# Experts on pairs of 256 slots with seven half-size products in a gated recurrence and mixture-of-experts kernel

## The chip, the cores and the metric

The kernel runs on one core of a Trainium2 chip. A core has a matrix engine (TensorE, PE in the profile), a vector engine (VectorE, DVE), a scalar engine (ScalarE, ACT), GpSimd (POOL) and a queue engine for transfers (SyncE, SP). They run side by side and wait for each other by semaphores. Matmul results go to PSUM, which has eight banks of 512 f32 columns on 128 partitions; everything else on the chip lies in SBUF. The metric is the device time of one execution in microseconds. All arithmetic is f32.

## The reference, cut to what matters

A gated linear recurrence over 768 steps makes 3072 rows of 384 features. A router picks two of eight experts for each row; each expert is a two-layer network, and its result is weighted and added.

```python
f = 1.0 / (1.0 + np.exp(-f_logit))                     # B, H, S, D = 4, 8, 768, 48
for t in range(S):
    state = f[:, :, t, :, None] * state + np.einsum('bhd,bhe->bhde', k[:, :, t], v[:, :, t])
    y[:, :, t] = np.einsum('bhd,bhde->bhe', q[:, :, t], state)
x = y.transpose(0, 2, 1, 3).reshape(B * S, H * D)       # 3072 x 384

noisy_logits = x @ w_gate + np.log1p(np.exp(x @ w_noise)) * noise
top2 = np.argpartition(-noisy_logits, 2, axis=1)[:, :2] # top2_w: softmax over the two
for e in range(E):                                      # E = 8, w1[e] 384 x 1024, w2[e] 1024 x 384
    for k in range(2):
        mask = top2[:, k] == e
        h = np.maximum(x[mask] @ w1[e], 0.0)
        out[mask] += top2_w[mask, k, None] * (h @ w2[e])
```

So there are 6144 slots (a row and one of its experts), and in the expert part almost all the arithmetic lies: 24 + 24 weight tiles of 128 x 128 per expert. On the given inputs the experts get 766, 738, 811, 777, 800, 755, 719 and 778 slots.

## The kernel before

The attention works through 24 steps (six chunks of 128 time steps for each of four batch rows). In every step VectorE, ScalarE and TensorE take turns; the loads of f, q, k and v go into rings of padded tiles:

```python
RING = {"f": 5, "q": 4, "k": 4, "v": 6}
pads = {n: [ld.tile([C, H, DP], F32, tag=f"{n}{i}", name=f"{n}{i}") for i in range(RING[n])] for n in "fqkv"}
```

The router of each chunk ranks the slots and writes each expert's list of slots to memory. After half of the chunks a first plan (`NA` = 17 blocks) and after all of them a second plan say which expert and which 128 slots each of the 48 blocks takes; four half blocks of 64 slots take what is left of a list. The first blocks begin while the attention's last steps still run. A block is this:

```python
def turned(t):
    xp = one_bank(f"xgp{t}")
    for i in range(KO):                                   # KO = 3
        nc.tensor.transpose(xp[:, i * 128:(i + 1) * 128], xg[t][:, i * 128:(i + 1) * 128], ident)
    xt[t] = ffn.tile([128, KO, 128], F32, tag="xt", name=f"xt{t}")
    nc.vector.tensor_copy(xt[t], xp[:, 0:DM].rearrange("d (k t) -> d k t", k=KO))

def block_of(t, end=NB - NT):
    ahead("fetch", min(t + 5, end))                       # slot lists of later blocks
    ahead("gather", min(t + 4, end))                      # their rows, by an indirect DMA
    hs = ffn.tile([128, FO, 128], F32, tag="hs", name=f"hs{t}")
    for half in range(2):
        hp = one_bank(f"hp{t}_{half}").rearrange("f (o t) -> f o t", t=128)
        for o in range(FO // 2):                          # FO = 8
            fo = half * (FO // 2) + o
            for i in range(KO):
                nc.tensor.matmul(hp[:, o, :], lhsT=w1[t % NR][:, i, fo * 128:(fo + 1) * 128],
                                 rhs=xt[t][:, i, :], start=(i == 0), stop=(i == KO - 1))
        nc.scalar.activation(hs[:, half * (FO // 2):(half + 1) * (FO // 2), :], hp, AF.Relu)
        # ... (the pieces take turns with other work: yield)
    ahead(1, min(t + NR + 1, end))                        # w1 of block t + 2, if its expert is another
    if t + 1 < end:
        turned(t + 1)
    yield
    yp = one_bank(f"yp{t}")
    for fo in range(FO):
        nc.tensor.matmul(yp[:, 0:DM], lhsT=hs[:, fo, :], rhs=w2[t % NR][:, fo, :],
                         start=(fo == 0), stop=(fo == FO - 1))
        # ...
    ahead(2, min(t + NR + 1, end))                        # w2 of block t + 2
    ys = ffn.tile([128, DM], F32, tag="ys", name=f"ys{t}")
    nc.vector.tensor_scalar(ys, yp[:, 0:DM], slots[t][:, 1:2].bitcast(F32), None, ALU.mult)
    nc.gpsimd.indirect_dma_start(out=out, out_offset=bass.IndirectOffsetOnAxis(ap=slots[t][:, 2:3], axis=0),
                                 in_=ys, in_offset=None, bounds_check=N - 1, oob_is_err=False, compute_op=ALU.add)
    yield
```

The last transfer scatters the block's weighted rows into `out` and adds them there. The half block does the same with 64 slots, on both column halves of TensorE, and ends in two scatters. A branch behind the main part takes what the plan could not place; on these inputs it isn't taken.

Of the kernel before, what the change touches and what calls it, by code (L numbers as in the profile page):

```python
# [331 lines left out]
def kernel(  # L332
# [37 lines left out]
    nc = tc.nc  # L370
# [10 lines left out]
    NB = max((2 * N - 65 * n) // 128 + n for n in range(E + 1))  # L381
    NH = 4
    HALF = NCH // 2
    NT = 3
    NA = -(-(2 * HALF * B * C - E * 127) // 128)
# [12 lines left out]
    ps2 = ctx.enter_context(tc.tile_pool(name="ps2", bufs=1, space=PSUM))  # L398
    ps1 = ctx.enter_context(tc.tile_pool(name="ps1", bufs=6, space=PSUM))
    wk = ctx.enter_context(tc.tile_pool(name="wk", bufs=2))  # L400
    ffn = ctx.enter_context(tc.tile_pool(name="ffn", bufs=3))
    loads = ExitStack()
    ld = loads.enter_context(tc.tile_pool(name="ld", bufs=1))

    def one_bank(name):
        return ps1.tile([128, 512], F32, tag="one", name=name)
# [10 lines left out]
    pads = {n: [ld.tile([C, H, DP], F32, tag=f"{n}{i}", name=f"{n}{i}") for i in range(RING[n])] for n in "fqkv"}  # L417
# [16 lines left out]
    end_of = counting("end_of", [[128, N // 128]], base=128)  # L434
    block = counting("block", [[1, NB]])

# [10 lines left out]
    LR = E * N + 128  # L447
# [42 lines left out]
    xw, puts = [], []  # L490
# [123 lines left out]
    def route(c):  # L614
# [63 lines left out]
        def put(b, r):  # L678
            into = nc.gpsimd.indirect_dma_start(  # L679
# [15 lines left out]
    steer, steer_h = {}, {}  # L695

    def plan(name, n, groups, count):


        def t(shape, tag, dtype=F32):  # L700
            return rt.tile([128] + shape, dtype, tag=tag, name=f"{tag}_{name}", bufs=1)

        total = one_bank(f"total_{name}")[:, 0:E]
        nc.tensor.matmul(total, lhsT=ones, rhs=upto[groups - 1][:, :, B], start=True, stop=True)
        full = t([E, N // 128], "full")
        nc.vector.tensor_tensor(full, total.unsqueeze(2).broadcast_to((128, E, N // 128)),
                                (end_of if count == ALU.is_ge else over_of).unsqueeze(1).broadcast_to((128, E, N // 128)), count)
        yield
        nblk, ends, step = t([E], "nblk"), t([E], "ends"), t([E], "step")
        nc.vector.tensor_reduce(nblk, full, axis=AX.X, op=ALU.add)  # L710
        if count == ALU.is_gt:
            half, first, ends_h = t([E], "half"), t([E], "first"), t([E], "ends_h")
# [30 lines left out]
        yield  # L743
        nc.vector.memset(new[:, 0:NR], 1.0)
        nc.vector.tensor_tensor(new[:, NR:], ex[:, NR:], ex[:, 0:n - NR], ALU.not_equal)
        nc.vector.tensor_copy(to[:, :, 2], new)
        yield
        if count == ALU.is_ge:

# [375 lines left out]
```

## Time and profile before

| what | value |
|---|---|
| time, median of three runs | 725.64 us (725.5 to 729.05) |
| span of the profiled execution | 730.0 us, mean TensorE clock 0.984 |
| first-layer matmuls (line 838), x2304 | 267.7 us |
| second-layer matmuls (line 849), x768 | 257.3 us |
| turning of gathered rows (line 816), x144 | 24.0 us |
| scatters into `out` (line 856), x48 | 76.0 us on GpSimd |
| weights, inputs and outputs through the hardware queue | 135.91 MB |

In the profile's lines a name such as L838 is a line of the kernel. A line of the slices gives for each fortieth of the span the busy share of an engine in tenths. A row of the timeline has the start, the duration, the engine, the line, the operation with its output and inputs, and how many instructions were merged; in brackets stands how long the engine had been idle and who ended that. A row by stretch of time gives the stretch, its length, the busy time of PE, of the weight loads, of DVE, ACT and POOL, then the clock, the share of the DMA engines that was busy, and GB/s. A row of waits gives who waited for whom, the sum in us, how many times, and the longest.

### The profile page before, as it was taken

How to read it: one execution, taken by the hardware profiler on the slowest of the kernel's cores; microseconds unless marked ns; L12 is line 12 of the kernel's file. 1: busy time of each engine (PE TensorE's matmuls, PEld its weight loads, DVE VectorE, ACT ScalarE, POOL GpSimd, SP SyncE). 2: the span in 40 equal slices, each digit the busy share in tenths (PEclk: the TensorE clock that was granted, in tenths of full speed). 3: DMA queues.
4: the chain of work that ended last, by engine and by line, in shares of the span. 5: the costliest groups of instructions: out<-in, count | busy, mean ns of one | idle time of the engine just before them, and what ended most of it. 6: DMA issues, size and time to landing. Idle time of an engine off the chain costs nothing.

```text
span 730.0 us, 13666 instructions
## 1 busy us (share of the span) xinstructions
PE 699.4 (96%) x5354; PEld 563.0 (77%) x5354; DVE 200.2 (27%) x503; ACT 163.7 (22%) x365; POOL 232.8 (32%) x267
## 2 busy tenths in 40 slices
PE   6999989969999999999999999999999999999992
PEld 5889978858788787787788768876787678767881
DVE  7878887822232250010110110010011001101000
ACT  5766655621111010110010011001110101010100
POOL 5223674421174562122132123312322232312210
PEclk9999999989999999999999999999999999999997
DMA  8889888889997988899839649974997189563211
GB/s 173 151 199 216 166 164 182 165 279 368 373 260 194 251 189 264 282 301 331 276 57 381 195 113 292 351 250 118 302 348 233 26 267 333 161 210 74 34 23 15
DMA packets 179866, 156.41 MB, mean 214 GB/s; under 512 B 116978, under 2 KB 164240, under 8 KB 179792
## 3 DMA queue, kind: packets, MB, share of 16 engines
q1 hardware_dynamic: 167440, 135.91, 62.7%
q0 software_dynamic: 12352, 19.52, 13.2%
q8 instruction: 45, 0.74, 0.4%
q14 instruction: 29, 0.24, 0.1%
HBM read 192.51 MB, written 20.15 MB: 291 GB/s over the span
## 4 chain that ended last, share of the span: by engine, by line
PE 87%; DMA 5%; DVE 3%; ACT 1%; SPq 1%; issue 1%; POOL 0%; POOLq 0%; DVEq 0%; ACTq 0%
PE hp L838 36%; PE yp L849 34%; PE sc L554 3%; PE xgp L816 2%; PE xp L605 2%; PE y L572 2%; PE yp_h L910 1%; PE hp_h L896 1%; DMA k<-in_k_dram 1%; DMA w<-in_moe_w_dram 1%; DMA x_rows<-xs 1%; PE y L583 1%; DVE L L528 1%; PE kp L514 1%; PE kp L548 1%
## 5 line engine op out<-in xcount | busy, mean ns | idle before, releaser
L838 PEld LDWEIGHTS hp<-xt,w 128*128 128x128 f32 x2304 | 264.9, 192 | 15.3 <-issue 3.4
L838 PE MATMUL hp<-xt,w 128*128 128x128 f32 x2304 | 267.7, 276 | 0.4 <-DMA w<-in_moe_w_dram 0.4
L849 PE MATMUL yp<-w,hs 128*128 128x384 f32 x768 | 257.3, 487 | 0.0
L849 PEld LDWEIGHTS yp<-w,hs 128*128 128x128 f32 x768 | 141.7, 190 | 90.0 <-issue 2.6
L856 POOL DMA_INDIRECT out_dram<-ys,slots x48 | 76.0, 1583 | 308.8 <-DVE ys L855 171.4
L840 ACT ACTIVATE hs<-hp 128x512 f32<-128x512 f32 x96 | 57.3, 597 | 455.1 <-PE hp L838 455.1
L818 DVE COPY xt<-xgp 128x384 f32<-128x384 f32 x48 | 26.8, 558 | 236.8 <-PE xgp L816 236.8
L855 DVE TENSOR_SCALAR ys<-yp,slots 128x384 f32<-128x384 f32 x48 | 29.6, 617 | 204.0 <-PE yp L849 199.4
L799 POOL DMA_INDIRECT xg<-x_rows,slots x48 | 47.9, 999 | 35.4 <-DMA slots<-lists 19.1
L679 POOL DMA_INDIRECT lists<-entry,sloti x48 | 47.6, 992 | 12.9 <-issue 9.1
L508 POOL TENSOR_SCALAR f<-f 128x384 f32<-128x384 f32 x22 | 28.0, 1272 | 30.8 <-DMA f<-in_f_logit_dram 17.4
L557 DVE TENSOR_TENSOR A<-sc,causal 128x1024 f32<-128x1024 f32 x24 | 29.3, 1222 | 16.1 <-PE sc L554 15.9
L554 PE MATMUL sc<-qP,kQ 64*128 64x128 f32 x384 | 30.6, 304 | 0.0
L528 DVE TENSOR_TENSOR_SCAN L<-f,cap 128x512 f32<-128x512 f32 x24 | 29.8, 1243 | 2.2 <-ACT cap L523 2.2
L572 PE MATMUL y<-A,v 128*64 128x128 f32 x384 | 28.1, 290 | 1.7 <-DMA v<-in_v_dram 1.4
L816 PE MATMUL xgp<-ident,xg 128*128 128x128 f32 x144 | 24.0, 276 | 5.5 <-DMA xg<-x_rows,slots 5.5
L915 POOL DMA_INDIRECT out_dram<-ys_h,slots_h x8 | 11.4, 1431 | 55.6 <-DVE ys_h L913 48.0
L554 PEld LDWEIGHTS sc<-qP,kQ 64*128 64x128 f32 x384 | 25.7, 204 | 4.3 <-issue 3.8
L605 PE MATMUL xp<-w_rt,yT 128*128 128x112 f32 x192 | 27.2, 284 | 0.0
L572 PEld LDWEIGHTS y<-A,v 128*64 128x64 f32 x384 | 21.9, 143 | 5.6 <-DVE A L557 1.6
L605 PEld LDWEIGHTS xp<-w_rt,yT 128*128 128x128 f32 x192 | 23.3, 191 | 3.6 <-issue 2.2
L587 ACT COPY yT<-y 128x256 f32<-128x256 f32 x48 | 15.5, 376 | 41.7 <-PE y L583 40.3
(169 smaller groups left out, 439.3 us busy)
## 6 DMA issues: line engine op xcount, KB each, us to landing
w<-in_moe_w_dram SPq DMA_DIRECT2D x96, 1536.0 KB
w_h<-in_moe_w_dram SPq DMA_DIRECT2D x8, 1536.0 KB
f<-in_f_logit_dram SPq DMA_DIRECT2D x24, 192.0 KB
q<-in_q_dram SPq DMA_DIRECT2D x24, 192.0 KB
k<-in_k_dram SPq DMA_DIRECT2D x24, 192.0 KB
v<-in_v_dram SPq DMA_DIRECT2D x24, 192.0 KB
x_rows<-xs SPq DMA_DIRECT2D x24, 192.0 KB
out_dram<-zero SPq DMA_DIRECT2D x24, 192.0 KB
```

Source lines behind the costliest of these rows:

```text
L528: nc.vector.tensor_tensor_scan(L[n], data0=logf[n], data1=cap[n % 2].rearrange("d a t -> d (a t)"), initial=0.0, op0=ALU.add, op1=ALU.min)
L554: nc.tensor.matmul(sc[:, par, cols(hp)], lhsT=kQ[n][rows(par), cols(hp)], rhs=qP[n][rows(par), cols(hp)], start=True, stop=True)
L572: nc.tensor.matmul(at(hp, par), lhsT=vt[:, 2 * hp + par, :], rhs=A[n][:, par, cols(hp)], start=(hp < 2), stop=(c == 0 and hp >= HP - 2))
L605: nc.tensor.matmul(xp[:, hp, :], lhsT=yT[n][:, hp % 2, cols(hp // 2)], rhs=w_rt[:, hp, :], start=True, stop=True)
L679: into = nc.gpsimd.indirect_dma_start(out=lists, out_offset=bass.IndirectOffsetOnAxis(ap=sloti[:, r, b:b + 1], axis=0), in_=entry[:, c, b, ...
L799: nc.gpsimd.indirect_dma_start(out=xg[t], out_offset=None, in_=x_rows[0:HALF * B * C] if t < NA else x_rows, in_offset=bass.IndirectOffset ...
L816: nc.tensor.transpose(xp[:, i * 128:(i + 1) * 128], xg[t][:, i * 128:(i + 1) * 128], ident)
L838: nc.tensor.matmul(hp[:, o, :], lhsT=w1[t % NR][:, i, fo * 128:(fo + 1) * 128], rhs=xt[t][:, i, :], start=(i == 0), stop=(i == KO - 1))
L840: nc.scalar.activation(hs[:, half * (FO // 2):(half + 1) * (FO // 2), :], hp, AF.Relu)
L849: nc.tensor.matmul(yp[:, 0:DM], lhsT=hs[:, fo, :], rhs=w2[t % NR][:, fo, :], start=(fo == 0), stop=(fo == FO - 1))
L855: nc.vector.tensor_scalar(ys, yp[:, 0:DM], slots[t][:, 1:2].bitcast(F32), None, ALU.mult)
L856: nc.gpsimd.indirect_dma_start(out=out, out_offset=bass.IndirectOffsetOnAxis(ap=slots[t][:, 2:3], axis=0), in_=ys, in_offset=None, bounds_ ...
```

## The change

Blocks of 128 slots become pairs of 256. The first layer keeps its 24 matmuls per pair, each with 256 columns, so that each weight tile is loaded into TensorE half as often. The second layer is a product of a 256 x 1024 by a 1024 x 384 matrix. It is cut in halves in each dimension, and the two-by-two product is formed with seven half-size products instead of eight (Winograd's form of Strassen's scheme), four matmuls of 192 columns each, with VectorE making four sums of hidden quarters (`sm`, S1 to S4), four of weight quarters (`u`) and eight sums of the products:

```diff
+        def mix(*which):
+            for m in which:
+                x, y, op = {"u1": (b(0, 1), b(0, 0), ALU.subtract), "u2": (b(1, 1), u[1], ALU.subtract),
+                            "u3": (b(1, 1), b(0, 1), ALU.subtract), "u4": (b(1, 0), u[2], ALU.subtract),
+                            "s1": (a(0, 1), a(1, 1), ALU.add), "s2": (sm[1], a(0, 0), ALU.subtract),
+                            "s3": (a(0, 0), a(0, 1), ALU.subtract), "s4": (a(1, 0), sm[2], ALU.subtract)}[m]
+                nc.vector.tensor_tensor((u if m[0] == "u" else sm)[int(m[1])], x, y, op)
+        when = [["u3"], ["u1"], ["u2", "s3"], ["u4"]] if t else [[], [], [], ["u3", "s3"]]
+        when += [["s1"], ["s2"], ["s4"]] if t else [["u1", "u2"], ["u4", "s1"], ["s2"]]
...
+        hs = ffn.tile([128, FO, 256], F32, tag="hs", name=f"hs{t}", bufs=1)
+        for fo in range(0, FO, 2):
+            hp = one_bank(f"hp{t}_{fo}").rearrange("f (o t) -> f o t", o=2)
+            for o in range(2):
                 for i in range(KO):
...
+                    nc.tensor.matmul(hp[:, o, :], lhsT=w1[t % NR][:, i, (fo + o) * 128:(fo + o + 1) * 128], rhs=xt[t][:, i, :],
+                                     start=(i == 0), stop=(i == KO - 1))
+            nc.scalar.activation(hs[:, fo:fo + 2, :], hp, AF.Relu)
+            mix(*when[fo // 2])
...
+        def product(name, x, y):
+            if len(P) % 2 == 0:
+                bank.append(one_bank(f"y{t}_{len(bank)}"))
+            P[name] = bank[-1][:, (len(P) % 2) * HC:(len(P) % 2 + 1) * HC]          # HC = 192
+            for o in range(FH):                                                     # FH = 4
+                nc.tensor.matmul(P[name], lhsT=x[:, o, :], rhs=y[:, o, :], start=(o == 0), stop=(o == FH - 1))
+        ys = [ffn.tile([128, DM], F32, tag=f"ys{s}", name=f"ys{t}_{s}", bufs=1) for s in range(2)]
...
+        def scatter(s):
+            nc.scalar.mul(ys[s], ys[s], slots[t][:, s, 1:2].bitcast(F32))
+            nc.gpsimd.indirect_dma_start(out=out, out_offset=bass.IndirectOffsetOnAxis(ap=slots[t][:, s, 2:3], axis=0),
+                                         in_=ys[s], in_offset=None, bounds_check=N - 1, oob_is_err=False, compute_op=ALU.add)
+        product(1, a(0, 0), b(0, 0));  mix(*when[4])                                # (lines joined here)
+        product(7, sm[3], u[3])
+        nc.scalar.copy(P17.rearrange("t a w -> t (a w)"), bank[0][:, 0:DM]);  turned(t + 1, 0);  mix(*when[5])
+        product(2, a(1, 0), b(1, 0));  mix(*when[6])
+        product(4, a(1, 1), u[4])
+        nc.vector.tensor_tensor(left[0], P17[:, 0], P[2], ALU.add)
+        nc.vector.tensor_tensor(left[1], P17[:, 1], P[4], ALU.add);  turned(t + 1, 1)
+        product(5, sm[1], u[1])
+        product(6, sm[2], u[2])
+        nc.vector.tensor_tensor(mid, P17[:, 0], P[6], ALU.add)
+        nc.vector.tensor_tensor(right[1], P17[:, 1], P[5], ALU.add)
+        nc.vector.tensor_tensor(left[1], left[1], mid, ALU.add)
+        nc.vector.tensor_tensor(right[1], right[1], mid, ALU.add)
+        scatter(1)
+        nc.vector.tensor_tensor(mid, mid, P[5], ALU.add)
+        product(3, sm[4], b(1, 1))
+        ahead(2, t + NR + 1)
+        nc.vector.tensor_tensor(right[0], mid, P[3], ALU.add)
+        scatter(0)
```

The eight sums are not given room of their own; they lie in the rings that held f, q and k, which are free once the attention's last loads are used:

```diff
+    f_all = ring.tile([C, RING["f"], H, DP], F32, tag="f_all", name="f_all")
+    qk_all = ring.tile([C, RING["q"] + RING["k"], H, DP], F32, tag="qk_all", name="qk_all")
+    sm = {i + 1: f_all[:, i].rearrange("p h d -> p (h d)").rearrange("p (o t) -> p o t", t=128) for i in range(4)}
+    u = {i + 1: qk_all.rearrange("p a h d -> p (a h d)")[:, i * FO // 2 * HC:(i + 1) * FO // 2 * HC].rearrange(
+        "p (o c) -> p o c", c=HC) for i in range(4)}
```

Therefore all but the first three pieces of the first pair wait for the last steps, and the first plan has five pairs (`NA`), the whole 24 (`NP`):

```diff
-            if early and stage not in (summed, decays):
-                next(blocks)
+            for _ in range(2 if i >= NS - 1 else 1):
+                if done[2] >= NR and (n_first < 3 or i >= NS - 2 and stage is not forget):
+                    next(pairs)
+                    n_first += 1
```

After the attention its PSUM pools are closed and one pool of eight banks takes their place (before: six single banks and one double one throughout). The plan makes pairs, single blocks and half blocks; the main part runs pairs and half blocks only, and single blocks would go to the branch behind it.

## The prediction

> **What bounds the kernel now.** I read the page's busy shares and slices first, to find the engine and the stages.
>
> ```profile
> PE 699.4 (96%) x5354; PEld 563.0 (77%) x5354; DVE 200.2 (27%) x503; ACT 163.7 (22%) x365; POOL 232.8 (32%) x267
> PE   6999989969999999999999999999999999999992
> DVE  7878887822232250010110110010011001101000
> PEclk9999999989999999999999999999999999999997
> ```
>
> TensorE (PE) is busy in nearly every slice at full clock. VectorE (DVE) is busy only in the first eight slices, which are the attention; after that it has room. A busy PE is not a PE at its peak, so I asked for TensorE's waits from 147 us on, and for busy times by stretch.
>
> ```profile
> PE xgp L816 <- DMA xg<-x_rows,slots: 5.5, 1, 5.5
> PE hp L838 <- DMA w<-in_moe_w_dram: 0.4, 1, 0.4
> ...
> 147.00:180.00 33.00, 27.09 (x250) 22.18 (x249) 7.34 (x21) 6.20 (x18) 3.94 (x4) 0.90 0.93 321
> ...
> 300.00:420.00 120.00, 120.00 (x743) 96.34 (x743) 13.62 (x24) 13.14 (x22) 29.27 (x23) 1.00 0.81 261
> 420.00:640.00 220.00, 220.00 (x1342) 167.28 (x1342) 23.81 (x43) 25.65 (x43) 60.47 (x47) 1.00 0.76 234
> ```
>
> From 147 us to the last matmul TensorE waits 5.9 us in all (the first two lines), just where the experts begin. So from 153 to 717 us the time is the sum of TensorE's work, and a change is worth what it takes off that sum, plus what it adds in waits. What one block costs is read from the starts in the timeline of two blocks.
>
> ```profile
> 310.45 5.52 PE L838 MATMUL hp<-xt,w 128*128 128x128 f32 x48
> ...
> 315.80 0.49 PE L816 MATMUL xgp<-ident,xg 128*128 128x128 f32 x3
> ...
> 316.13 5.33 PE L849 MATMUL yp<-w,hs 128*128 128x384 f32 x16
> ...
> 321.29 5.52 PE L838 MATMUL hp<-xt,w 128*128 128x128 f32 x48
> ```
>
> Start to start: first layer 315.80 - 310.45 = 5.35 us, turning the next rows 0.33, second layer 321.29 - 316.13 = 5.16; a block is 10.84 us, two are 21.68. One matmul of the program is two instructions here (24 give x48, 8 give x16), so an instruction takes 5.35/48 = 111.5 ns with 128 columns and 5.16/16 = 322.5 ns with 384.
>
> [...] the transposes show (0.33/3 = 110 ns), while the first layer shows 111.5. [...] the trace has 689 ns for the 128x512 product of line 540. [...] Here every scatter into `out` is ordered that way, and the trace shows it between the two scatters of a half block:
>
> ```profile
> 434.91 1.43 POOL L915 DMA_INDIRECT out_dram<-ys_h,slots_h  x1 [12.01 <-DVE ys_h L913]
> 438.41 1.41 POOL L915 DMA_INDIRECT out_dram<-ys_h,slots_h  x1 [2.07 <-DMA out_dram<-ys_h,slots_h]
> ```
>
> **The change part by part.**
>
> *Amount of work.* On these inputs the eight lists hold 766, 738, 811, 777, 800, 755, 719 and 778 slots. Three pairs serve each, the last one where it has over 192 slots to take; 811, 777, 800 and 778 leave 43, 9, 32 and 10, which are half blocks; no expert leaves a single block. So 24 pairs and four half blocks replace 48 blocks and four half blocks, and the slow branch at the end stays untaken.
>
> *First layer.* 24 matmuls a pair, now with 256 columns: 48 instructions x [...] = 10.36 us, against 2 x 5.35 = 10.70. Off: 0.34 us.
>
> *Second layer.* Seven products of four matmuls with 192 columns: 56 instructions x [...] = 9.10 us, against 10.32. Off: 1.22 us, a little less than an eighth[...]. The six transposes stay, 0.66 us.
>
> So a pair is 20.12 us instead of 21.68: 1.56 us less, times 24 = 37.4 us off TensorE. Half blocks and attention keep their matmuls.
>
> *VectorE.* Per pair: four sums of w2 quarters [...], four of hidden quarters [...], eight sums of products [...], two copies of turned rows at the trace's 558 ns (1.12 us). Sum 10.6 us[...], in 20.1: 53%, beside TensorE. On ScalarE four Relu of 597 ns, a copy and two scalings at about 476 ns (128x384, line 610): 3.8 us. GpSimd: two gathers at 999 ns and two scatters at 1583 ns, 5.2 us, as before for two blocks.
>
> *Do the sums come in time?* From the end of the first layer a product is 1.30 us. The Relu and S1 end at about 0.7 + 0.7 = 1.4 us and S1 is first used by the fifth product at 5.9. S2 waits behind the first turned copy (2.9 to 3.5) and ends near 4.2; it is used at 7.2. S4 ends near 4.9 and is used at 8.5. The sums of w2 and S3 go beside the next pair's first layer: 4 x 0.96 + 0.69 = 4.5 us in 10.4. I find no stop in the steady state.
>
> *Weights.* A set is loaded when it differs from that of two pairs ago: 21 times against 30, 3.1 MB each, 28 MB less. Each half of a set (w1, w2) has 20 us or more to land; the first one took 150.97 to 159.87 us.
>
> *The start.* Blocks start at 153 us now, as the attention's last steps run. The first pair comes at nearly the same place, its slot lists a few slots earlier, but it needs two gathers and operand rings that the attention has just left. I put down 2 us more idle time, bubbles of the first pairs included.
>
> *The tail.*
>
> ```profile
> 717.23 0.62 DVE L855 TENSOR_SCALAR ys<-yp,slots 128x384 f32<-128x384 f32 x1 [9.90 <-PE yp L849]
> 718.12 1.56 POOL L856 DMA_INDIRECT out_dram<-ys,slots  x1 [8.96 <-DVE ys L855]
> ```
>
> Now one scatter goes out 0.9 us after the last matmul. After the change two do. The first needs four sums (about 1.3 us) and a scaling (0.5) after the sixth product, with handovers about 2.5 us, and takes at least 4.2 us to land (the fastest landing of line 856). The second may go only then: 6.7 us after the sixth product, or 5.4 after the seventh. The tail grows by 4.5 us.
>
> Sum: 725.6 - 37.4 + 2 + 4.5 = 694.7; I say 695.
>
> **Rivals.** (a) *VectorE sets the pace.* [...] it would be half busy where it was about a tenth busy (13.62 of 120 us). Against it stand the margins of 2 us or more above. One microsecond lost a pair would cost 24: 719, nothing gained worth the name. (b) *The start eats it.* VectorE is still 70 to 80% busy in the attention, and the first pair's eight sums stand in the same queue; the half used rings and banks change hands just there. Ten more microseconds idle would give 703. (c) *Scatters or weights take over.* Pairs 0 to 14 each bring a new set, 3.1 MB in 20 us, and at four of them a half block's 3.1 MB comes on top: about 310 GB/s, where slices of the page show up to 381. A pair with a half block has four scatters in a chain, at the median 7.2 us near 28 us, and the result tiles have one buffer. Three microseconds at each of the four would give 707. (d) *The tail doesn't grow or the start stall vanishes:* 688 to 690.
>
> **Range and chances.** The saving is counted from measured spacings, so I trust it within 2 us; what I don't know is the waits, and they lie on the slow side more than on the fast one. 80%: 687 to 707. Faster by over 2% means below 711.1; only (a), or several rivals together, spoil that.
>
> **What would show it.** First-layer matmuls x1152 spaced 216 ns, products x1344 spaced 162.5 ns, a steady pair of 20.1 us; TensorE's last matmul near 682 us; the last scatter waiting some 4 us for the one before it; VectorE near half busy after 180 us. The prediction is wrong if the pair is longer than 20.6 us, or if TensorE waits more than 10 us for VectorE's sums, ring, weights or gathers after 150 us.

## The result, and the profile after

The changed kernel takes 753.82 us (median of four executions, 751.33 to 754.86) where the kernel before takes 727.35: a ratio of 1.0357, with a 95% interval of 1.0311 to 1.0403. It is slower by 26 us; 695 us, 32 us faster, had been predicted. The profiled execution spans 751.5 us.

The shares and slices of the changed kernel's page, to be held against those of before:

```profile
PE 677.7 (90%) x4778; PEld 605.6 (81%) x4778; DVE 375.9 (50%) x860; ACT 204.6 (27%) x437; POOL 248.1 (33%) x266
PE   5899999829999887999999799969998999999990
DVE  7578879723637562445442444235335445544440
PEclk9899999979999989999999899979999999999996
```

TensorE's busy time fell by 22 us (699.4 to 677.7), although part of it was worked at a lower clock (0.958 on average against 0.984). But the slices are no longer all nines: there are holes in slices 9 (150 to 169 us), 14 to 17, 23, 27 and 31. VectorE is half busy, as the sums make it. The saving is there; time without work has been put beside it.

Two pairs late in the kernel, from TensorE's timeline:

```profile
634.15 10.52 PE L872 MATMUL hp<-xt,w 128*128 128x256 f32 x48
644.51 1.46 PE L886 MATMUL y<-w,hs 128*128 128x192 f32 x8
...
650.37 2.77 PE L886 MATMUL y<-qk_all,f_all 128*128 128x192 f32 x16
652.97 1.46 PE L886 MATMUL y<-w,f_all 128*128 128x192 f32 x8
654.27 10.52 PE L872 MATMUL hp<-xt,w 128*128 128x256 f32 x48
```

From one first layer to the next it is 654.27 - 634.15 = 20.12 us, the predicted figure to the last digit: 10.36 us of first layer, 1.30 for each product. An instruction takes 10.36/48 = 215.8 ns with 256 columns and 1.30/8 = 162.5 with 192; two of 192 take 325.0 where one of 384 took 322.5. The predicted 216 and 162.5 ns were my estimate, not measured spacings. A straight line through what the trace of before shows, 110 ns with 128 columns (the transposes) and 322.5 with 384, gives nearly the same estimate: 216.3 and 163.1 ns, a pair of 20.2 us. So the pair itself isn't where the prediction failed. Nor are the sums' durations, from the page's groups:

```profile
L860 DVE TENSOR_TENSOR f_all<-hs 128x512 f32<-128x512 f32 x48 | 33.2, 691 | 129.8 <-ACT hs L874 129.8
...
L860 DVE TENSOR_TENSOR qk_all<-w,qk_all 128x768 f32<-128x768 f32 x48 | 45.8, 954 | 0.8
```

The trace of before has 689 ns for a product of 512 columns (line 540) and 1222 for one of 1024 (line 557); half way between them, an estimate for 768 columns, is 956. With eight sums of products of 0.35 us and two copies of 0.56, VectorE's work for a pair is 10.5 us in 20.12, where the prediction has 10.6. The tail, too, is as foreseen: here are VectorE's last sum and the last two scatters.

```profile
734.64 0.35 DVE L931 TENSOR_TENSOR ys<-mid,y 128x192 f32<-128x192 f32 x1
...
735.12 1.56 POOL L894 DMA_INDIRECT out_dram<-ys,slots  x1 [11.49 <-ACT ys L893]
740.24 1.56 POOL L894 DMA_INDIRECT out_dram<-ys,slots  x1 [3.56 <-DMA out_dram<-ys,slots]
```

From the start of the last matmul to the end of the span it is 751.5 - 733.9 = 17.6 us, before 730.0 - 716.7 = 13.3: 4.3 us more, of which 4.5 were predicted.

What is wrong is when the last matmul starts: 733.9 us, not near 682. TensorE's waits from 147 us on say for whom:

```profile
PE hp L872 <- DVE xt L833: 24.6, 4, 9.9
PE xgp L832 <- DMA xg<-x_rows,slots: 10.0, 2, 5.1
PE count L1046 <- DVE low L1042: 3.5, 1, 3.5
PE y L886 <- DVE f_all L860: 1.3, 1, 1.3
```

These are 39 us in eight stops (three shorter ones, 2 us together, are left out), where the kernel before had 5.9. Almost none of it is for the operand sums (the last line). The longest row is for the copy of turned rows into `xt`: a plain copy, in three of the four stops late because a sum ahead of it on VectorE had itself stood waiting, for 9.00, 11.07 and 5.96 us. To see where the stops lie I divided each trace into four stretches: up to the first pair's first matmul, the first five pairs (ten blocks before), from there to the last matmul, and the tail. A row is one execution: that of `x_all` took 714.0 us (median of five 710.1), that of `x_w1` 705.1 (median of four 707.8), so a few us between two rows can belong to the execution and not to the kernel.

| kernel (one profile each) | first pair starts | five pairs | the rest | last matmul | tail |
|---|---|---|---|---|---|
| before | 159.9 | 118.0 | 438.8 | 716.7 | 13.3 |
| before, second trace | 162.9 | 121.8 | 438.8 | 723.5 | 13.2 |
| changed | 169.7 | 134.8 | 429.4 | 733.9 | 17.6 |
| changed, second trace | 164.7 | 131.3 | 431.4 | 727.4 | 17.9 |
| two result buffers (`x_ys2`) | 172.1 | 133.4 | 408.7 | 714.2 | 17.8 |
| and earlier plan (`x_plan`) | 170.9 | 127.3 | 408.7 | 706.9 | 17.7 |
| two buffers, paced writes (`x_pace`) | 160.8 | 132.6 | 408.7 | 702.1 | 18.1 |
| two buffers, both (`x_both`) | 167.7 | 126.5 | 408.7 | 702.9 | 18.1 |
| two buffers, ordinary product (`x_plain`) | 171.1 | 124.3 | 431.8 | 727.2 | 12.9 |
| two buffers, rings moved (`x_align`) | 161.3 | 129.4 | 408.7 | 699.4 | 17.8 |
| changed, rings moved (`a_align`) | 157.5 | 126.0 | 426.6 | 710.1 | 17.9 |
| before, rings moved (`x_shift`) | 166.8 | 118.0 | 438.8 | 723.6 | 13.0 |
| all four mends (`x_all`) | 158.1 | 126.7 | 408.7 | 693.5 | 18.2 |
| all four, ordinary product (`x_allplain`) | 157.2 | 128.8 | 431.7 | 717.7 | 12.9 |
| all four, first weights earlier (`x_w1`) | 152.7 | 123.6 | 408.7 | 685.0 | 18.2 |

In the third stretch 438.8 - 408.7 = 30.1 us can be saved, 1.58 for each of its 19 pairs, about the 1.56 predicted; the changed kernel lost 20.7 of them again. In the second it lost 16.8 us against before where 5 x 1.56 = 7.8 should have been won, and it started 9.8 us late. (Three attention steps lie behind the first pair's start, where two lay behind the first block's: 48 matmuls of line 577 in that stretch against 32 of line 572. So some 5 us of TensorE's work have moved from the first stretch to the second, and the first is late by more than it looks.) In all three there is something to look for.

### The profile page after: what moved, and what is told of

Same layout as the page of the kernel before. It is cut to its first block, busy times and chain, and to the rows that moved or that the text cites. A ratio compares the mean times of both kernels' runs of the same rounds, so it can differ in the third digit from the quotient of the medians.

```text
span 751.5 us, 12564 instructions
## 1 busy us (share of the span) xinstructions
PE 677.7 (90%) x4778; PEld 605.6 (81%) x4778; DVE 375.9 (50%) x860; ACT 204.6 (27%) x437; POOL 248.1 (33%) x266
## 3 DMA queue, kind: packets, MB, share of 16 engines
q1 hardware_dynamic: 154096, 107.60, 52.1%
q0 software_dynamic: 12352, 19.52, 13.2%
## 5 line engine op out<-in xcount | busy, mean ns | idle before, releaser
L872 PE MATMUL hp<-xt,w 128*128 128x256 f32 x1152 | 261.4, 387 | 25.7 <-DVE xt L833 24.6
L872 PEld LDWEIGHTS hp<-xt,w 128*128 128x128 f32 x1152 | 222.2, 194 | 58.1 <-DVE xt L833 25.7
L886 PE MATMUL y<-qk_all,f_all 128*128 128x192 f32 x576 | 104.2, 330 | 1.3 <-DVE f_all L860 1.3
L886 PEld LDWEIGHTS y<-qk_all,f_all 128*128 128x128 f32 x576 | 94.9, 192 | 5.0 <-issue 3.4
L886 PE MATMUL y<-w,hs 128*128 128x192 f32 x384 | 71.8, 331 | 0.0
L886 PEld LDWEIGHTS y<-w,hs 128*128 128x128 f32 x384 | 64.3, 193 | 1.5 <-issue 0.2
L685 POOL DMA_INDIRECT lists<-entry,sloti x48 | 50.8, 1058 | 10.5 <-issue 9.7
L860 DVE TENSOR_TENSOR qk_all<-w,qk_all 128x768 f32<-128x768 f32 x48 | 45.8, 954 | 0.8
L860 DVE TENSOR_TENSOR qk_all<-w 128x768 f32<-128x768 f32 x48 | 44.0, 952 | 0.0
L886 PE MATMUL y<-qk_all,hs 128*128 128x192 f32 x192 | 37.1, 338 | 0.0
L886 PE MATMUL y<-w,f_all 128*128 128x192 f32 x192 | 35.7, 329 | 0.0
L912 DVE TENSOR_TENSOR ys<-P,y 128x192 f32<-128x192 f32 x24 | 8.5, 354 | 50.2 <-DMA out_dram<-ys,slots 30.5
```

Of the source, the lines that this page charges most:

```text
L685: into = nc.gpsimd.indirect_dma_start(out=lists, out_offset=bass.IndirectOffsetOnAxis(ap=sloti[:, r, b:b + 1], axis=0), in_=entry[:, c, b, ...
L860: nc.vector.tensor_tensor((u if m[0] == "u" else sm)[int(m[1])], x, y, op)
L872: nc.tensor.matmul(hp[:, o, :], lhsT=w1[t % NR][:, i, (fo + o) * 128:(fo + o + 1) * 128], rhs=xt[t][:, i, :], start=(i == 0), stop=(i == K ...
L886: nc.tensor.matmul(P[name], lhsT=x[:, o, :], rhs=y[:, o, :], start=(o == 0), stop=(o == FH - 1))
```

## Experiments

### The two kernels again

The kernel before and the changed one were run once more without an edit, to see what of their traces repeats.

> The kernel before once more, beside the others. If the late semaphores (in the changed kernel's trace increments of TensorE, VectorE and ScalarE are seen up to 12 us after the instruction that makes them ended, always while GpSimd writes slot lists) belong to the changed program, this trace has none, as the first trace of before had none: lag under 0.1 us, span near 730 us. If they belong to the chip or the day, they show here too, at the list writes of 70 to 135 and 200 to 265 us.

> The changed kernel once more. If its stops are its own, TensorE stops again for about 10 us near 160 us, 5 us for gathered rows near 290 us, and 5 to 8 us after the half blocks; time 751 to 755 us. If the stop near 160 us was chance, it is gone and the time is near 742.

One execution of each: 738.46 us before, 747.45 after; the median of the kernel before beside them was 735.53 (23 executions), some 8 us more than in the first comparison. Beside that median the changed kernel's one execution is 1.016, not 1.036: a part of the first difference came from the conditions of the two measurements, and one execution can't say how much. The stops after half blocks and at the sixth pair's rows came back within about 1 us (6.3, 6.9, 2.5 and 5.1 us). The one ahead of the first pair did not: 3.0 us instead of 9.9.

And a thing I had taken for a doing of the change was now in the kernel before. The trace records when each semaphore's count changes, and some of these records come late beside the end of the instruction that raises the count. Two things must be told apart here. In the traces concerned about a tenth of the records is missing (1669 for 1827 raising instructions in the first trace of the changed kernel, 1307 for 1475 in the second trace of before), and where one is missing, the next one looks like its late arrival. The largest gaps, 12.3 us in the changed kernel and 10.8 in the kernel before, are of this kind: the instruction that waited had begun 0.03 us after the raising one's end. But other signals are late in fact, since the waiting instruction starts only when the record comes: 4.7 us late in the kernel before (raised at 242.4 us, a copy on VectorE begins at 247.1), 9.2 us in the changed one, and 10.6 in the one with two buffers below. In the first trace of before there is no such lag over 0.3 us. So late signals are no part of the change. Where they fall is.

### The half blocks: one buffer or two for the result tiles

The first trace of the changed kernel, around the pair that follows a half block (its timeline; columns as before):

```profile
485.73 1.57 POOL L894 DMA_INDIRECT out_dram<-ys,slots  x1 [7.67 <-issue]
...
493.11 0.35 DVE L912 TENSOR_TENSOR ys<-P,y 128x192 f32<-128x192 f32 x1 [11.07 <-DMA out_dram<-ys,slots]
493.38 0.35 DVE L913 TENSOR_TENSOR ys<-P,y 128x192 f32<-128x192 f32 x1
493.65 0.55 DVE L833 COPY xt<-xgp 128x384 f32<-128x384 f32 x1
...
494.25 8.02 PE L872 MATMUL hp<-xt,w 128*128 128x256 f32 x22 [7.30 <-DVE xt L833]
```

It is read from the bottom up. TensorE waited 7.3 us for the copy of the next pair's turned rows. The copy stood in VectorE's queue behind two sums of products (L912, L913), and the first of these waited 11.07 us for a scatter: it writes the result tile that the pair before was still sending out, because there is one buffer of each. The half block had put two more scatters into the chain (at 469.76 and 476.64 us), so the last one of the pair before went out only at 485.73 and the tile came free late. What the row of waits calls a wait for VectorE is a wait for a DMA, two steps back. And this stop cost more than itself. By stretches of the same trace, clock in the third column from the right:

```profile
476.00:486.00 10.00, 10.00 (x64) 9.83 (x63) 2.54 (x4) 1.08 (x2) 1.69 (x2) 1.00 0.76 275
494.30:498.30 4.00, 4.00 (x10) 3.16 (x11) 3.83 (x9) 1.23 (x2) 2.06 (x1) 0.50 0.97 304
```

The clock, 1.00 ahead of the stop, is granted at 0.50 for the 4 us after it, and at 0.74 over the next 4. Behind the stop of 5.23 us at 412 us it is 0.50 over 4 us as well; behind the one of 2.19 us at 564 us it is 1.00.

```diff
-        ys = [ffn.tile([128, DM], F32, tag=f"ys{s}", name=f"ys{t}_{s}", bufs=1) for s in range(2)]
+        ys = [ffn.tile([128, DM], F32, tag=f"ys{s}", name=f"ys{t}_{s}", bufs=2) for s in range(2)]
```

> Changed kernel with two buffers for each result tile instead of one. Theory A: the four scatters of a pair with a half block go one after the other, the next pair's sums wait for the tile, and TensorE for VectorE (15.7 us of stops at 412, 487 and 564 us, and some 6 us more at half clock after them): these go, time 728 to 735. Theory B: the chain of scatters itself is too long and the wait only moves to the pair after: gain under 8 us, time 745 to 752.

Measured: 734.23 us, 0.9926 of the kernel before (0.989 to 0.9963). In the table the third stretch is 408.7 us instead of 429.4 and 431.4: 21 to 23 us, at three places. Behind the first three half blocks the pairs of the changed kernel's first trace had lost 7.8, 10.6 and 2.4 us (8.3, 10.1 and 4.4 in its second), behind the fourth nothing; why that one went free stays open. From 300 us on TensorE's list of waits is empty, and the pair with a half block runs without a break:

```profile
455.80 2.80 PE L982 MATMUL yp_h<-w_h,hts_h 128*64 128x384 f32 x16
458.53 1.57 PE L886 MATMUL y<-w,f_all 128*128 128x192 f32 x8
459.93 10.52 PE L872 MATMUL hp<-xt,w 128*128 128x256 f32 x48
```

The cause of these stops is shown. In time the gain is smaller: beside the changed kernel's 747.45 us it is 13 us, for in the trace with two buffers the stop ahead of the first pair was 11.3 us and not 3.0. One word brought the change from a loss to about a break-even.

### The first five pairs: a second plan that comes late

In the changed kernel the rows of the sixth pair came so late that TensorE stood for 4.94 us:

```profile
278.68 3.62 SPq L804 DMA_DIRECT2D slots<-lists  x4
...
286.76 1.59 POOL L894 DMA_INDIRECT out_dram<-ys,slots  x1 [5.90 <-ACT hs L874]
...
288.66 1.02 POOL L815 DMA_INDIRECT xg<-x_rows,slots  x1 [0.30 <-issue]
...
295.67 0.88 PE L832 MATMUL xgp<-ident,xg 128*128 128x128 f32 x3 [4.94 <-DMA xg<-x_rows,slots]
```

The slot lists of four pairs are fetched together at 278.7 us, as soon as the second plan is there, and the gather that needs one of them then stands on GpSimd behind a scatter that begins only 5.90 us after the end of the scatter before it. The first plan has five pairs, no more than this. In `x_plan` (two buffers as well) the plan's work is taken up faster and its last count is left until later:

```diff
-        yield
-        yield
+        for _ in range(6):
+            yield
...
-        for _ in range(2):
+        for _ in range(4):
             next(router, None)
+        for _ in range(2):
             if puts:
                 puts.pop(0)()
```

> Two buffers for the result tiles, and the second plan's work comes earlier: four router steps per piece instead of two, and six pieces are left between the second plan's small VectorE operations and the count that TensorE makes of them. Theory A (the second plan is late, so that pair 5's lists and rows are late): with two buffers alone the rows of pair 5 cost 5.4 us near 290 us and the count 3.8 us near 268 us[...]; both stops should be gone and the time 8 to 10 us below that of two buffers alone, 0.980 of the kernel before. Rival B (the rows are late because GpSimd is full of scatters and writes of slot lists, however early the plan is): the stop near 290 us only moves or splits, and the time is within 3 us of two buffers alone, 0.992.

Four executions took 718.54 to 733.51 us, median 728.34, with 734.3 for the kernel before beside them: too wide for a ratio. Its trace tells more. The stop at the sixth pair is gone (waits for gathered rows 4.6 us in all, at the start, instead of 9.5), and the five pairs take 127.3 us instead of 133.4. The wait for the count I had expected to go as well: it only moved, from 268 to 247 us, and is 3.9 us long instead of 3.5. Half of the step was right.

### The start: signals that come late

In the first trace of the changed kernel, from the turning of the first pair's second half to its first matmul:

```profile
159.32 0.55 PE L832 MATMUL xgp<-ident,xg 128*128 128x128 f32 x3
159.49 0.97 POOL L685 DMA_INDIRECT lists<-entry,sloti  x1 [0.22 <-issue]
...
169.12 0.56 DVE L833 COPY xt<-xgp 128x384 f32<-128x384 f32 x1 [11.88 <-remote]
...
169.73 2.50 PE L872 MATMUL hp<-xt,w 128*128 128x256 f32 x5 [9.86 <-DVE xt L833]
```

The transposes end at 159.9 us; the copy, which waits for nothing else that the trace shows, begins 9.2 us later. The counts that TensorE had raised at 159.4 to 159.9 us are recorded at 168.98 to 169.09, and the copy begins 0.03 us after the last of them. In these 9 us GpSimd writes slot lists to memory (L685), 16 bytes for each of 128 slots, eight writes of about 1 us back to back from 156.9 to 166.8. The kernel before does the same writes, but from 204 us on, amid blocks; in its second trace, with signals late there too, TensorE waited 2.5 us for ScalarE. `x_pace` (two buffers as well) holds the later chunks' writes until the first pair has begun, and puts a copy of one word of the newest ScalarE result ahead of each:

```diff
+            if paced:
+                nc.gpsimd.tensor_copy(spacer, paced[-1])
...
+            paced.append(hs[0:1, fo, 0:1])          # after each Relu; likewise after the copy of P1 and P7
...
-        while len(steer) < NA or puts:
+        while len(steer) < NA or len(n_put) < HALF * B * 2:
```

> Two buffers for the result tiles, and the writes of later chunks' slot lists by GpSimd are held until the first pair has begun and then each waits for a word of the latest result of ScalarE, so that they no longer go out back to back. Theory A (signals between the engines arrive late while GpSimd writes slot lists one right after another, and the first pair's handshakes fall into such a run): the stop of 10 to 12 us near 160 us is gone or below 3 us, and the time 8 to 12 us below that of two buffers alone, 0.978 of the kernel before. Rival B (the stop at the first pair is VectorE's own queue, full with the attention's last steps): the stop stays within 3 us of what it was and the time within 3 us of two buffers alone, 0.992.

In its trace the first pair starts at 160.8 us instead of 172.1, and what is left of the stop is a wait for something else:

```profile
155.99 0.52 PE L835 MATMUL xgp<-ident,xg 128*128 128x128 f32 x3 [0.63 <-DMA xg<-x_rows,slots]
160.84 5.12 PE L875 MATMUL hp<-xt,w 128*128 128x256 f32 x12 [4.32 <-DMA w<-in_moe_w_dram]
```

The span fell by 11.8 us (732.0 to 720.2), but the ratio is 0.9913 (0.9881 to 0.9946) and hardly differs from the 0.9926 of two buffers alone. The ratio compares each kernel's fastest executions, and says little of a disturbance that only some have. What speaks for the mechanism besides the trace is the spread: two buffers alone took 725 to 742.6 us (20 executions, in another set than the paced kernel's), the paced kernel 722.9 to 729.4 (four). I call it supported by the trace and not shown by the time. In `x_align`, further down, the same order of writes went with no lag over 0.3 us from 100 to 300 us, and this stop was absent without any pacing. That back-to-back writes make the signals late is thus not shown. What makes them late at one time and not at another stays open too: in each of the four sets of kernels that ran one after the other, all traces had them or none did. In the first comparison the trace of before had none and that of the changed kernel had them.

Both mends together, with fetches and gathers of the second plan's pairs allowed as soon as the last list is written, and not before, and with one list written per piece of a pair where there were two:

```diff
+            if t >= NA and (what == "fetch" and len(n_put) < NCH * B * 2 or what == "gather" and t not in slots):
+                return
...
+        ahead("fetch", t + 5)
+        ahead("gather", t + 3)
```

> Two buffers, the earlier second plan and the paced writes of slot lists together. If the three causes are separate they add: about 20 us below two buffers alone, 0.970 of the kernel before, with TensorE's last matmul near 695 us and the steady pair still 20.1 us. If pacing the writes makes the second plan late again, the stop at pair 5's rows comes back and the time is only that of the better of the two, 0.980.

Measured: 721.06 us, 0.9811 (0.9775 to 0.9847), TensorE's last matmul at 702.9 instead of near 695. Better than either, less than the sum: the first pair started at 167.7, 6.9 later than in the paced kernel. Of this about 5 us were lost in the attention up to 118 us, with a signal 5.9 us late at 114; the wait for the first weights (4.8 us) was about the same in both (4.3 in the paced kernel).

### What the seven products are worth

`x_plain` has two buffers and pairs of 256, but the second layer as the ordinary product, without any sum:

```diff
-            mix(*when[fo // 2])
...
+        for s in range(2):
+            yp = one_bank(f"yp{t}_{s}")
+            # in four and three pieces, with the next pair's rows turned between them
+                    nc.tensor.matmul(yp[:, 0:DM], lhsT=hs[:, fo, s * 128:(s + 1) * 128], rhs=w2[t % NR][:, fo, :],
+                                     start=(fo == 0), stop=(fo == FO - 1))
+            nc.vector.tensor_scalar(ys[s], yp[:, 0:DM], slots[t][:, s, 1:2].bitcast(F32), None, ALU.mult)
+            # and the scatter of ys[s], as before
```

> Two buffers for the result tiles and pairs of 256, but the second layer as the ordinary product: eight matmuls of 384 columns for each 128 slots, no operand sums, no sums of products. By the spacings a pair is 10.36 + 10.32 + 0.66 = 21.34 us, 1.22 more than with seven products, 24 x 1.22 = 29 us over the run with two buffers, less 4 us of tail: plus 25 us. Theory A (the sums cost TensorE nothing outside the start and the tail): the time is 22 to 29 us above two buffers alone, about 1.027 of the kernel before. Rival B (the sums hold TensorE up in the start and after each disturbance): the start stop of 11 us and the one near 260 us go with them, and the time is only 8 to 15 us above two buffers alone, about 1.007.

Measured: 738.59 us, 1.0032 (1.0001 to 1.0063), only about 8 us above two buffers alone: rival B's number. The table says why. In the third stretch the ordinary product takes 431.8 us against 408.7, 23.1 longer, 1.22 for each of 19 pairs, just as counted. In the first five pairs it takes 124.3 against 133.4, though its pairs are longer: VectorE is freer when the second plan's small operations come (busy 33.0 us of these 124.3, against 67.6 of 134.8 in the changed kernel), and the stops at the count, at the sixth pair's rows and near 258 us don't occur. So the sums did cost time, in the first five pairs, by filling VectorE while the plan was made. Is it so in any case, or only as long as the plan is late? That is asked again below, when a fourth cause is out of the way.

### The attention's first 35 us: where the load rings lie

The change leaves the attention as it is, and yet its third step comes 6 us later. TensorE's rows of that step, before and after:

```profile
29.20 1.09 PE L572 MATMUL y<-A,v 128*64 128x128 f32 x16
```

```profile
35.28 1.49 PE L577 MATMUL y<-A,v 128*64 128x128 f32 x15
```

The loads of f, q, k and v are slow. By stretches of time, 5 to 20 us, the last two columns being the DMA engines' share and GB/s; before, then after:

```profile
5.00:20.00 15.00, 12.83 (x117) 11.27 (x116) 11.50 (x21) 9.56 (x23) 6.46 (x9) 0.89 0.90 173
```

```profile
5.00:20.00 15.00, 10.87 (x91) 8.30 (x91) 11.10 (x21) 9.68 (x23) 5.60 (x9) 1.00 1.50 163
```

Fewer bytes with 1.7 times the DMA time: packets of the same 192 bytes that began between 6 and 18 us took 15.5 ns on average before and 27.9 after (15.3 and 27.7, the figures of the expectation below, with the few smaller packets of that time). The rings now lie elsewhere in SBUF. Before they begin at byte 189760 of each partition, which is 64 past a multiple of 256; after at 121824, which is 224 past one. Each row of 192 bytes has a place of 256, so all rows of a kernel lie alike to a multiple of 256. That this place makes the packets slow was my guess at this point. What the time of a packet is made of, no run here shows.

Two kernels test it: `x_align` moves the rings of the kernel with two buffers by 32 bytes, to 124928, a multiple of 256 (the second buffers had moved them by 3072 already, where the first loads move 163 GB/s at a share of 1.49, as in the changed kernel); `x_shift` moves those of the kernel before by 32 bytes, to 96 past a multiple. In `x_shift` nothing but the rings moves; in `x_align` most other tiles of the attention and the pairs move by the same 32 bytes, so `x_shift` is the cleaner test.

```diff
+    ffn.tile([128, 8], F32, tag="spare", name="spare", bufs=1)      # x_align: ahead of the rings' pool
     ring = ctx.enter_context(tc.tile_pool(name="ring", bufs=1))
...
+    ld.tile([128, 8], F32, tag="spare", name="spare")               # x_shift: first in the rings' pool
     pads = {n: [ld.tile([C, H, DP], F32, tag=f"{n}{i}", name=f"{n}{i}") for i in range(RING[n])] for n in "fqkv"}
```

> Two buffers for the result tiles, and 32 unused bytes per partition ahead of the load rings, so that the rings of f, q, k and v begin at a multiple of 64 bytes, as in the kernel before, and not 32 bytes behind one; nothing else. Theory A (the rings' place makes each 192-byte row of a load slower: in the first 20 us a packet took 27.7 ns on average against 15.3 before, the loads moved 163 GB/s against 202, and the attention's third step came 6 us later): packets back at 15 ns, the third step at about 29 us instead of 35, the first pair 5 to 6 us earlier, the time 5 to 6 us below that of two buffers alone, 0.985 of the kernel before. Rival B (the loads are slow because they now share two tiles and wait for each other): packets and time as with two buffers alone, 0.992.

> The kernel before with its load rings moved by 32 bytes per partition, nothing else. Theory A (the place): packets of the first 20 us rise from 15 to about 28 ns, the attention's third step moves from 28-29 to about 35 us and the time rises by 4 to 6 us, 1.007 of the kernel before. Rival B: the time is the same, 1.000.

The same stretch in `x_align`, and in `x_shift`:

```profile
5.00:20.00 15.00, 12.98 (x117) 11.49 (x116) 11.50 (x21) 9.67 (x23) 6.70 (x9) 1.00 0.89 172
```

```profile
5.00:20.00 15.00, 12.02 (x86) 9.53 (x86) 10.94 (x21) 9.29 (x21) 5.57 (x9) 0.89 1.53 164
```

Packets took 15.6 ns in `x_align` and 28.6 in `x_shift`; the attention's third step came at 28.6 and 33.1 us. `x_shift` took 737.96 us, 1.0101 of the kernel before (1.0062 to 1.014): 32 bytes, in a kernel otherwise untouched, cost 7 us, and in the table all of it lies ahead of the first block (166.8 against 159.9). `x_align` took 714.15 us, 0.9775 (0.9742 to 0.9807), 11 us below two buffers alone, by the two ratios. Six of these are the attention's; the rest I can't ascribe, since the late signals were absent this time and other tiles moved as well. I had spoken of multiples of 64. The four places measured, counted from a multiple of 256 (15.6 ns at 0, 15.5 at 64, 28.6 at 96, 27.9 at 224), agree with that, but four places don't settle a rule. The runs do rule out that the rings are slow because they share two tiles: in `x_align` they share them too.

### All together, and the ordinary product once more

`x_all` is the kernel of both mends with the 32 bytes; `x_allplain` the same with the ordinary second layer of `x_plain`.

> Two buffers, the earlier second plan, the paced writes of slot lists, and the rings at a multiple of 64 bytes. If the four causes are separate: 5 to 6 us below the run without the last of them (0.981), that is 0.973 of the kernel before, with TensorE's last matmul near 697 us. If the time gained in the attention is lost again in waiting for the first weights and rows: within 2 us of 0.981.

> As the run with all four mends, but the second layer as the ordinary product (eight matmuls of 384 columns for each 128 slots, no operand sums). By the spacings it is 24 x 1.22 = 29 us longer, less 4 of tail: 25 us over the run with all four, 1.006 of the kernel before. Theory A (in the run with only two buffers the ordinary product lost just 4 us because it escaped the stops near 260, 268 and 290 us): now that these are mended, 18 to 25 us over the run with all four. Rival B (VectorE's sums cost the first pairs time whatever is mended): only 8 to 12 us over it.

`x_all`: 710.1 us, 0.9733 (0.9701 to 0.9766), as expected, last matmul at 693.5. `x_allplain`: 732.86 us, 1.0042 (1.0015 to 1.0069). The difference is 0.0309 of 729 us, 22.5 us: theory A. The five pairs now take 126.7 with the sums and 128.8 without, 2.1 of the 6.1 us that five pairs should gain; behind them the gain is as counted (431.7 against 408.7). So the seven products give nearly what was counted once the rest is out of the way. And the pairs of 256 alone, with everything mended, give nothing over the kernel before.

### One cause alone, and the wait that is left

`a_align` is the changed kernel with the 32 bytes and nothing else. `x_w1` is `x_all` with the first pair's w1 asked for after one slot list:

```diff
-        for what, until in (("", 1), ("fetch", 2), ("fetch", 4), (1, 1), ("fetch", 5), (2, 1), ("", 7), ("gather", 1),
+        for what, until in (("", 1), ("fetch", 1), (1, 1), ("fetch", 4), ("fetch", 5), (2, 1), ("", 7), ("gather", 1),
```

> The changed kernel with 32 unused bytes per partition ahead of the load rings and nothing else (result tiles with one buffer, plan and slot lists as they were). Theory A (the causes are separate and add): the rings' place is worth 11 us here as it was with two buffers, so 1.036 becomes 1.021 of the kernel before, with the three stops after half blocks (about 6, 7 and 3 us) still there. Rival B (the 11 us were in part a lucky meeting of the first pair with two buffers): the gain is only the 5 to 6 us that the attention lost, 1.028.

> The run with all four mends, with the first pair's w1 asked for right after the first slot list and not after the fourth. TensorE waits 4.4 us for it there. Theory A (the transfer goes out too late): the wait falls below 1.5 us and the time by 3 to 4 us, 0.969 of the kernel before. Rival B (the transfer shares the DMA engines with the attention's last loads and with the gathers, which then come later): the wait moves to the gathered rows and the time stays within 1.5 us, 0.973.

`a_align`: 733.53 us, 1.0074 (1.0047 to 1.0101), lower than both had it. Its stops after half blocks are still there (third stretch 426.6), its start and five pairs are as with all mends: here, too, no signal was late. It has neither the earlier plan nor the paced writes, and takes 157.5 and 126.0 us where `x_all` takes 158.1 and 126.7; `x_align` and `x_all` differ by 0.004, within their intervals. That these two mends are worth anything where signals come on time is thus not shown. So of the changed kernel's 1.0357 about 0.028 went; the place of the rings accounts for 0.010 of it by `x_shift`, and the rest is most likely the absence of late signals, which this run can't separate from the other tiles' 32 bytes. `x_w1`: 707.83 us, 0.9725 (0.9696 to 0.9754). The wait for the weights is gone; TensorE's longest waits after 145 us are now

```profile
PE xgp L836 <- DMA xg<-x_rows,slots: 4.8, 1, 4.8
PE count L1056 <- DVE low L1052: 3.9, 1, 3.9
```

The first pair starts at 152.7 us instead of 158.1, but the first rows are waited for 4.8 us instead of 3.1 (both theories in part): the waits ahead of it fall by some 2 us only, the attention's last steps came 2 to 3 us earlier, and by the intervals the time can't be told from `x_all`'s. It has the lowest ratio of the study, 20 us (0.0275 of 729) below the kernel before.

## Why the prediction was wrong, step by step

**Right.** The steady pair (20.12 predicted and measured); the sums' durations and that they come in time in the steady state, with a VectorE wait for one of them of 1.3 us in the whole kernel, in the fourth pair; the weights (28 MB less: 107.60 MB through the hardware queue against 135.91); the tail (4.5 predicted, 4.3 measured). Of the steps that were meant to show it, all came true but one, "TensorE's last matmul near 682 us", and the condition for being wrong, more than 10 us of waits after 150 us, was met nearly four times over.

**Wrong: the waits, three terms of the sum.** In `x_w1` the last matmul starts at 685.0 us, 3 us from the prediction; from it to the changed kernel's 733.9 are 48.9 us, which the table splits:

- *"I put down 2 us more idle time, bubbles of the first pairs included"*, for the start. The first pair starts 17.0 us later than in `x_w1` (169.7 against 152.7), the five pairs take 11.2 us more (134.8 against 123.6). What lies in them: the place of the load rings, about 6 us, shown by `x_shift`; the copy that came 9.2 us late, in an execution with late signals (3.0 us in the second); the wait for the first weights, 4 to 5 us where that stop was gone, of which an earlier request took away some 2; the rows of the sixth pair, 5 us, by a plan that came too late; the count, 3.5 us (3.9 with the earlier plan, 0.9 in `x_align`, where signals were on time); and half-clock time after the stops. All but the first are sizes from single traces, and they overlap. My rival (b) had the place right (rings and banks "change hands just there") and gave it ten microseconds.
- *"Three microseconds at each of the four would give 707"*, in rival (c). I had seen both facts, four scatters in a chain and one buffer for the result tiles, had them 28 us long against a pair of near 20, and left the term out of the sum. It is the largest single one: 20.7 us, 7.8, 10.6 and 2.4 behind three of the half blocks and nothing behind the fourth. The chain's length was right; what I missed is that the sum of products that is held for a result tile (11.07 us at 493 us) stands on VectorE ahead of the copy that TensorE needs next, and that the clock stood at 0.50 in the 4 us behind the stops of 5.2 and 7.3 us.
- *"Half blocks and attention keep their matmuls"*: true, and I took from it that the first 147 us stay as they are. I read no place of any buffer. The rings of f, q and k went into another pool so that the sums could lie in them; every ring, that of v too, came to lie elsewhere, and a packet of a row took 27.9 ns where it had taken 15.5.

The mechanism of the saving was right and its size was right (22.5 us measured between `x_all` and `x_allplain`, 25 counted). What failed is the assumption behind the sum, that a kernel bound by one engine stays so when its neighbours' buffers, queues and places are changed: each of the three is outside the part that I counted.

## What to carry to other kernels

When a change is meant to shorten the bound engine's work, count what the other engines' queues carry at the few irregular places (first units, half units, plan boundaries), not only in the steady state, and follow a wait back through the queue of the engine that it names until it ends at a DMA or a buffer. A buffer that is merely moved is a change too: compare the rates of the first loads before and after. And try the cheap mend first: a second buffer (21 to 23 us of the table's third stretch) and 32 bytes (7 us in the kernel before), which cost no instruction, were worth more than the 22 us that seven products save.

## What the runs showed of the hardware that I had not expected

- Moving the destination of 192-byte rows by 32 bytes changed the mean time of a packet from 15.5 to 28.6 ns in the kernel before and brought it from 27.9 in the changed one to 15.6 in `x_align`.
- In some traces a waiting instruction started up to 10.6 us after the instruction that signals it had ended (two buffers, at 171 us), with the semaphore's count recorded as changing only then, often while GpSimd was writing lists of 16-byte entries back to back; in `x_align` no lag was over 0.3 us from 100 to 300 us. The kernel before took 735.5 and 734.3 us beside kernels with the lag and 728.9 and 729.2 beside those without. What sets it was not found.
- The traces with the lag miss about a tenth of the records of semaphore counts, those without it next to none. A late record therefore shows a late signal only where the waiting instruction starts with it.
- Behind a stop of 7.3 us the clock was halved for about 6 us (0.50 over 4 us, then 0.74 over the next 4). Behind a stop of 3.5 us, TensorE's wait for the count, it was 0.50 from 268.3 to 275.1 us in the changed kernel's first trace and 1.00 with two buffers: the length of a stop alone doesn't decide it.
